# Spectral filter and MLP in one kernel: the real channel folded into the tables, GpSimd's sums taken out, stage 1 and the inverse tables reordered

## The chip, the cores and the metric

The kernel runs on one core of one Trainium2 chip. The metric is device microseconds (us) of one execution, the median of the timed runs. A run has a state; runs over 1.5% above the fastest of the same kernel count as slow, and verdicts and ratios use fast runs alone. That rule turns out to matter here, because the kernel before has two kinds of execution 1.6% apart, for a reason that an experiment below shows.

## The reference

Two blocks with a layernorm ahead of each. The first is a 2-D real FFT of a 2048 x 512 input, a product with complex weights, and the inverse transform; the second is an MLP with a squared ReLU (D = 512, F = 1792).

```python
def _A_ref(x, w_r, w_i):
    X = jnp.fft.rfft2(x.astype(jnp.float32), axes=(-2, -1))
    X = X * (w_r + 1j * w_i)                      # 2048 x 257 complex
    return jnp.fft.irfft2(X, s=(2048, 512), axes=(-2, -1)).astype(jnp.bfloat16)

def _B_ref(x, w1, b1, w2, b2):
    h = x @ w1 + b1
    r = jnp.where(h > 0, h, 0)
    return (r * r) @ w2 + b2

h = x + _A_ref(_layernorm(x), A_w_r, A_w_i)
h2 = h + _B_ref(_layernorm(h), B_w1, B_b1, B_w2, B_b2)
```

A real FFT of 512 points has 257 channels, of which channels 0 and 256 are real. That is one channel too many for 256 complex slots. The kernel before keeps channels 0 to 255 in the slots, leaves the imaginary table of channel 0 at zero and packs the two real channels 0 and 256 into slot 0, which therefore needs a different product from all the others.

## The kernel before

The transforms are matmuls with sine tables made on the chip. Stage 1 (with the layernorm folded into the table `KFr`) and stages 2 and 3 go forward, `spectral` multiplies with the weights, stages 4, 5 and 6 go back; then the MLP runs in five chunks (the "dense part"). The parts that the argument touches:

```python
def ln1_fold(a, b):                                   # layernorm's 1/std into stage 1's table
    for g in range(a, b):
        nc.vector.tensor_scalar(KFr[:, g, :], KF[:], rs1[:, g:g + 1], None, ALU.mult)

def real_products(e, a, b):                           # slot 0: its own products, on GpSimd
    ...
    nc.gpsimd.tensor_tensor(ta[:], SD[:, e], a.unsqueeze(1).to_broadcast([P, 2, 2]), ALU.mult)
    nc.gpsimd.tensor_tensor(tb[:], SD[:, e], b.unsqueeze(1).to_broadcast([P, 2, 2]), ALU.mult)

def real_sums(t, p_out, m_out):                       # ... and sums of 2 elements per partition
    ta, tb = t
    nc.gpsimd.tensor_tensor(p_out, ta[:, 0], tb[:, 1], ALU.subtract)
    nc.gpsimd.tensor_tensor(m_out, ta[:, 1], tb[:, 0], ALU.add)

def spectral(pr):                                     # VectorE: 8 instructions per pair of rows
    ...
    for m, w in ((mA, WB[0]), (mB, WB[1])):
        nc.vector.tensor_tensor(m[:], X[:], w[:, pr:pr + step + 1:step, 0:256]..., ALU.mult)
    ...
    prods = real_products(pr, AB[:, 0, :, 0], AB[:, 1, :, 0])
    nxt[0]()                                          # half of the next pair's butterfly
    nc.vector.tensor_tensor(Z[:, :, 0], mA[:, :, 0], mB[:, :, 1], ALU.subtract)
    nc.vector.tensor_tensor(Z[:, :, 1], mA[:, :, 1], mB[:, :, 0], ALU.add)
    nxt[1]()
    nc.vector.tensor_tensor(M[:, 0], Z[:, 0], Z[:, 1], ALU.add)
    nc.vector.tensor_tensor(M[:, 1], Zf[:, 3::-3], Zf[:, 1:3], ALU.subtract)
    real_sums(prods, M[:, 0, :, 0], M[:, 1, :, 0])    # GpSimd overwrites slot 0 of M

def table_i(*ks):                                     # inverse tables: transpose, copy, negate
    tr = mm_tile("ptr", BF16)
    ...                                               # TensorE transposes EF into tr
    nc.scalar.copy(EI[:, sl, 0:2, :], tr[...])
    if ks[0] == 0: ...                                # KI too
    else: nc.vector.tensor_scalar(EI[:, sl, 2, :], EI[:, sl, 0, :], -1.0, None, ALU.mult)

for pr in range(9):
    if 0 < pr and pr + 2 < 8: stage3(pr + 2)
    if pr + 3 < 8:            stage2(pr + 3)
    if pr > 0:                stage4(pr - 1, split=(pr == 8))     # reads Z and M
    if pr >= 5:               warm(mm_tile("idle")[:, 0:512], 5)
    if pr < 8:                spectral(pr)
    if pr < 3:                table_i(*((0, 8), (1, 2, 3), (4, 5, 6, 7))[pr])
    ...
```

The names: U is stage 2's result and AB stage 3's, each copied from TensorE's output by ScalarE. VectorE's butterfly makes X from AB (sums and differences of the pair's two rows; pair 0 needs none); mA and mB are X times the real and the imaginary weights; Z and M combine them, and stage 4 reads M (for pair 0 also Z). T is stage 4's result. EF and GF are the sine tables of the way forward, EI, KI and GI those of the way back. X, Z and M have two buffers each. KFr is stage 1's table times rs, the layernorm's 1/std.

In the trace before, ScalarE's copies come in the order of this loop (T at 35.13 us, the table EI at 36.04, AB at 36.73), so the place of `table_i` in it is also its place in ScalarE's row.

Of the kernel before, what the change touches and what calls it, by code (L numbers as in the profile page):

```python
# [15 lines left out]
P = 128  # L16
# [18 lines left out]
def kernel(  # L35
# [16 lines left out]

# [32 lines left out]
    SD = fwd.tile([P, 9, 2, 2], FP32, name="SD")  # L85
# [60 lines left out]
    def w_reversed(i):  # L146
# [5 lines left out]
    w_reversed(0)  # L152
# [22 lines left out]
    w_reversed(1)  # L175
    nc.gpsimd.memset(mhalf[:], -0.5)
    nc.gpsimd.iota(idxL[:].rearrange("p (r e j) -> p r e j", r=2, e=2), pattern=[[0, 2], [1, 2], [2, 128]], base=0,
                   channel_multiplier=0)
    nc.gpsimd.memset(idxL[:, 256:257], 256)

    def angles_g(t):
        o = 512 * t
        nc.gpsimd.tensor_scalar(fiG[:, o:o + 257], idxL[:, 0:257], cols[:, t:t + 1], float(QT), ALU.mult, ALU.add)
        nc.gpsimd.tensor_scalar(fiG[:, o + 257:o + 512], idxL[:, 257:512], cols[:, t:t + 1], float(HT),
                                ALU.mult, ALU.add)
# [33 lines left out]
    def ln1_fold(a, b):  # L219
        for g in range(a, b):  # L220
            nc.vector.tensor_scalar(KFr[:, g, :], KF[:], rs1[:, g:g + 1], None, ALU.mult)  # L221

    def stage1(g0, n=0, split=False):
        if split:
            pts = [mm_tile("p1a")[:, 0:512], mm_tile("p1b")[:, 0:512]]
        else:
            pt = mm_tile("p1")
            pts = [pt[:, 0:512], pt[:, 512:1024]]
# [11 lines left out]
        if split:  # L240
            for t, cp in ((0, nc.scalar.copy), (1, nc.vector.tensor_copy)):
                cp(dst[:, 2 * t:2 * t + 2], pts[t].rearrange("p (e i q s) -> p e i q s", e=2, i=2, q=16))  # L242
        else:
            nc.scalar.copy(dst, pt[:].rearrange("p (e i q s) -> p e i q s", e=4, i=2, q=16))  # L244
# [12 lines left out]
    ln1_sums(7)
    angles_g(0)
    ln1_rstd(2, 6)
    ln1_stats(6, 8, 9)  # L260
    ln1_fold(2, 6)
    angles_g(1)
    stage1(2)
    ln1_rstd(6, 10)
    nc.gpsimd.memset(ident[:], 0.0)
    nc.gpsimd.affine_select(out=ident[:], in_=ident[:], compare_op=ALU.not_equal,
                            fill=1.0, base=0, pattern=[[-1, P]], channel_multiplier=1)
    stage1(4)
    ln1_stats(10, 11)
    ln1_fold(6, 10)  # L270
    ln1_rstd(10, 12)
    sin_of(GF[:].rearrange("p t c -> p (t c)"), fiG[:])
    stage1(6)
    ln1_stats(12, 13)
# [20 lines left out]
    def w_real():  # L295

        for e in (0, 8):
            nc.gpsimd.tensor_scalar(SD[:, e, 0, :], WB[0][:, e, 0::256], 0.5, 1.0, ALU.mult, ALU.mult)
            nc.gpsimd.tensor_scalar(SD[:, e, 1, :], WB[1][:, e, 0::256], -0.5, 1.0, ALU.mult, ALU.mult)
        n_r, n_i = (w[:, 1:8, 0::256] for w in WB)  # L300
        v_r, v_i = (w[:, 22:15:-1, 0::256] for w in WB)
        nc.gpsimd.tensor_tensor(SD[:, 1:8, 0, :], n_r, v_r, ALU.add)
        nc.gpsimd.tensor_tensor(SD[:, 1:8, 1, :], v_i, n_i, ALU.subtract)
        nc.gpsimd.tensor_scalar(SD[:, 1:8], SD[:, 1:8], 0.5, 1.0, ALU.mult, ALU.mult)


# [381 lines left out]
```

## Time and profile before

| | us |
|---|---|
| median of 3 runs (188.0, 190.91, 191.0) | 190.91 |
| span of the profiled execution | 189.2 |
| VectorE's first product with the weights (mA of pair 0) | 26.25 |
| VectorE's last M of the spectral part ends | 59.39 |
| first stage 5 matmul (dense part begins) | 61.94 |
| from there to the end | 127.3 |

Rows of a timeline read: start, duration, engine, line, operation, output<-inputs and their shapes, count; in brackets the idle time of the engine just before and what ended it. PE is TensorE, PEld its weight loads, DVE VectorE, ACT ScalarE, POOL GpSimd. A duration can overlap the next instruction's start a little (an X of 0.42 us, and Z 0.34 us after its start), so VectorE's real pace is read from start to start. The "granted clock" is TensorE's clock as a share of full speed.

### The profile page before, as it was taken

The numbers are of one execution on the slowest core, as the hardware profiler recorded it, in microseconds if no ns is written. First come the engines' busy times: TensorE is split into PE (matmuls) and PEld (weight loads), VectorE is DVE, ScalarE is ACT, GpSimd is POOL, SyncE is SP. The second block draws the span as 40 slices with busy tenths as digits, with TensorE's granted clock in tenths as the row PEclk, the third lists the DMA queues.
The fourth block names the chain that finished last, engine by engine and source line by source line (L and its number), as shares of the span: only waits on it lengthen the run. The fifth ranks groups of instructions, "written<-read, shape, count | busy, mean of one in ns | idle before, by whom it ended". The sixth has DMA issues, their size and how long they took to land.

```text
span 189.2 us, 2712 instructions
## 1 busy us (share of the span) xinstructions
PE 160.5 (85%) x935; PEld 89.5 (47%) x948; DVE 124.1 (66%) x302; ACT 100.4 (53%) x169; POOL 63.2 (33%) x127
## 2 busy tenths in 40 slices
PE   3486876983499878799999899999999989999992
PEld 1154654752254447536563355444554434556440
DVE  7898479299686737764789526698436885449421
ACT  4768676995183427714791327860527850348300
POOL 7876946027753024020430202430204332016000
PEclk9999999999799999999999999999999999999999
DMA  5999970000000000001000100000010000110010
GB/s 163 351 410 412 368 179 10 0 0 3 0 2 0 0 0 3 0 2 48 11 0 0 44 12 28 3 0 28 28 59 2 0 0 28 54 35 0 0 55 29
DMA packets 7773, 11.19 MB, mean 59 GB/s; under 512 B 2256, under 2 KB 6224, under 8 KB 7504
## 3 DMA queue, kind: packets, MB, share of 16 engines
q1 hardware_dynamic: 7600, 10.11, 15.6%
q0 software_dynamic: 160, 0.92, 1.2%
q8 instruction: 7, 0.11, 0.3%
q14 instruction: 6, 0.05, 0.1%
HBM read 8.93 MB, written 2.10 MB: 58 GB/s over the span
## 4 chain that ended last, share of the span: by engine, by line
PE 52%; DVE 19%; ACT 16%; POOL 9%; issue 3%; POOLq 0%; ACTq 0%; DVEq 0%
PE ph L593 21%; PE po L612 19%; POOL M L317 3%; DVE act L597 3%; ACT U L341 3%; PE p L496 3%; ACT AB L367 2%; DVE hs L511 2%; ACT rl L596 2%; PE p L555 2%; DVE st L520 2%; ACT Bt L244 2%; ACT T L432 2%; ACT junk L517 1%; POOL rs L528 1%
## 5 line engine op out<-in xcount | busy, mean ns | idle before, releaser
L593 PE MATMUL ph<-UT,W 128*128 128x384 bf16 (+2 forms) x278 | 53.0, 336 | 0.8 <-ACT UT L559 0.5
L596 ACT ACTIVATE rl<-ph,b1f 128x384 bf16<-128x384 f32 (+2 forms) x70 | 41.2, 603 | 20.9 <-PE ph L593 19.5
L612 PE MATMUL po<-W,act 128*128 128x512 bf16 x217 | 49.9, 379 | 0.4
L597 DVE TENSOR_TENSOR act<-rl 128x384 bf16<-128x384 bf16 (+2 forms) x70 | 32.5, 478 | 17.2 <-ACT rl L596 16.8
L600 POOL TENSOR_TENSOR hb<-hs,b2b 128x512 f32<-128x512 bf16 x16 | 18.4, 1153 | 57.4 <-DVE act L597 55.4
L593 PEld LDWEIGHTS <-W 128*128 128x128 bf16 x280 | 27.3, 98 | 20.8 <-issue 1.4
L612 PEld LDWEIGHTS <-act 128*128 128x128 bf16 x224 | 21.6, 98 | 27.3 <-issue 3.1
L616 DVE TENSOR_TENSOR ot<-po,hb 128x512 bf16<-128x512 f32 x16 | 11.0, 690 | 18.1 <-PE po L612 18.1
L540 ACT ACTIVATE u<-hs,nm,rs 128x512 bf16<-128x512 bf16 x6 | 4.7, 809 | 25.2 <-DVE nm L537 25.2
L235 PE MATMUL p<-KFr,xs 128*128 128x256 bf16 x28 | 8.5, 330 | 5.1 <-DVE KFr L221 5.1
L424 PE MATMUL p<-EI,M 128*128 128x256 bf16 x28 | 7.2, 288 | 5.6 <-POOL M L317 5.4
L317 POOL TENSOR_TENSOR M<-ta,tb 128x2 bf16<-128x2 f32 x7 | 7.7, 1101 | 11.4 <-DVE M L406 11.2
L432 ACT CAST T<-p 128x1024 bf16<-128x1024 f32 x7 | 7.3, 1037 | 7.6 <-PE p L425 7.6
L511 DVE SCALAR_TENSOR_TENSOR hs<-p,xs 128x512 bf16<-128x512 f32 x16 | 10.8, 679 | 0.1
L496 PE MATMUL p<-GI,T 128*128 128x256 bf16 x64 | 9.4, 272 | 0.4 <-DVE T L430 0.4
L210 DVE BATCH_NORM_STATS2 st<-xs 128x6 f32<-128x512 bf16 x14 | 9.0, 673 | 0.6 <-DMA xs<-in_A_x_dram 0.6
L244 ACT CAST Bt<-p 128x1024 bf16<-128x1024 f32 x7 | 6.9, 1014 | 4.5 <-PE p L237 4.5
L249 PE MATMUL idle<-ones 128*128 128x512 bf16 x36 | 8.9, 379 | 0.1
L334 PE MATMUL p<-GF,Bt 128*128 128x256 bf16 x64 | 8.1, 273 | 0.8 <-ACT Bt L242 0.8
L510 PE MATMUL p<-R,KI 128*128 128x512 bf16 x16 | 6.1, 380 | 3.2 <-DVE R L506 3.1
L237 PE MATMUL p<-KFr,xs 128*128 128x256 bf16 x28 | 8.7, 335 | 0.0
L527 POOL TENSOR_SCALAR rs<-mv 128x3 f32<-128x3 f32 (+2 forms) x5 | 1.2, 240 | 22.3 <-DVE mv L521 22.2
(153 smaller groups left out, 237.0 us busy)
## 6 DMA issues: line engine op xcount, KB each, us to landing
W<-in_B_w_dram SPq DMA_DIRECT2D x2, 1792.0 KB, 19.0
out_dram<-ot SPq DMA_DIRECT2D x16, 128.0 KB, 1.8
xs<-in_A_x_dram SPq DMA_DIRECT2D x3, 512.0 KB, 6.9
WB<-in_A_w_r_dram SPq DMA_DIRECT2D x1, 1028.0 KB, 12.1
WB<-in_A_w_i_dram SPq DMA_DIRECT2D x1, 1028.0 KB, 12.9
xs<-in_A_x_dram SPq DMA_DIRECT2D x2, 256.0 KB, 3.5
b2b<-in_B_b_dram SPq DMA_DIRECT2D x1, 128.0 KB, 8.3
WB<-in_A_w_r_dram,idxR POOLq DMA_INDIRECT x1, 9.2
```

The source lines that it names most:

```text
L210: nc.vector.bn_stats(st[:], xs[:, g, :])
L244: nc.scalar.copy(dst, pt[:].rearrange("p (e i q s) -> p e i q s", e=4, i=2, q=16))
L317: nc.gpsimd.tensor_tensor(p_out, ta[:, 0], tb[:, 1], ALU.subtract)
L432: nc.scalar.copy(dst, src)
L496: nc.tensor.matmul(pe[:, 256 * e:256 * e + 256], lhsT=T2[:, lt, g].rearrange("p q s -> p (q s)"), rhs=GI[:, lt, :], start=(r == 0), stop=( ...
L511: nc.vector.scalar_tensor_tensor(hs[:, g, :], py[:], WSC, xs[:, g, :], ALU.mult, ALU.add)
L593: nc.tensor.matmul(ph[:, 0:n], lhsT=W1[:, d, bass.ts(f, P)], rhs=UT[:, d, 0:n], start=(d == 0), stop=(d == ND - 1))
L596: nc.scalar.activation(rl[:, 0:n], ph[:, 0:n], ACT.Relu, bias=b1f[:, f:f + 1], scale=1.0)
L597: sq = nc.vector.tensor_tensor(act[:, f, 0:n], rl[:, 0:n], rl[:, 0:n], ALU.mult)
L600: add = nc.gpsimd.tensor_tensor(hb[:, g, :], hs[:, g, :], b2b[:], ALU.add)
L612: nc.tensor.matmul(po[:], lhsT=act[:, f, bass.ts(i, P)], rhs=W2[:, f, :], start=(f == 0), stop=(f == NF - 1))
L616: nc.vector.tensor_tensor(ot[:], po[:], hb[:, g, :], ALU.add)
```

## The change

Its intent: use channels 1 to 256 as the 256 slots, so that channel 256 is an ordinary slot (its table column is halved) and channel 0, which the layernorm's mean subtraction makes zero on the input side, needs none. Then slot 0 needs no product of its own, and GpSimd leaves the spectral part. In the same edit stage 1 is reordered, one more group's statistics go to ScalarE (three instead of two), two folds go to GpSimd, and the inverse tables are copied earlier. Not shown in this excerpt: as the slots shift by one, even and odd channels swap places in the matmuls of stages 2 and 5. The diffs here are condensed; some put several lines into one.

```diff
-    w_reversed(0)                                   # gathers of the reversed weight rows, on GpSimd
+    nc.gpsimd.iota(idxL[...], ..., base=1, ...)     # channels 1 to 256
 ...
-def ln1_fold(a, b):
+def ln1_fold(a, b, eng=nc.vector):
 ...
     ln1_sums(3)
+    ln1_sums(7)
     ln1_stats(0, 1)
     ln1_rstd(0, 2)
+    w_reversed(0)
 ...
-    ln1_sums(7)
+    ln1_sums(11)
     angles_g(0)
     ln1_rstd(2, 6)
+    w_reversed(1)
 ...
     ln1_rstd(6, 10)
+    ln1_fold(8, 10, nc.gpsimd)
+    angles_g(1)
     stage1(4)
-    ln1_stats(10, 11)
-    ln1_fold(6, 10)
+    ln1_stats(10, 12)
+    ln1_fold(6, 8)
 ...
-    nc.vector.memset(GF[:, :, 0:1], 0.0)
+    nc.vector.tensor_scalar(GF[:, :, 255:256], GF[:, :, 255:256], 0.5, None, ALU.mult)
-    stage1(14, split=True)
+    tr08 = stage1(14, split=True)                   # free half of its PSUM buffer
+    transposed(tr08, (0, 8), True)
+    nc.scalar.copy(KI[:], tr08[:, 4 * P:5 * P])
+    table_i(tr08, (0, 8))
 ...
-    def w_real(): ...
-    def real_products(e, a, b): ...
-    def real_sums(t, p_out, m_out): ...
 ...
-            nc.vector.tensor_tensor(m[:], X[:], w[:, pr:pr + step + 1:step, 0:256]..., ALU.mult)
+            nc.vector.tensor_tensor(m[:], X[:], w[:, pr:pr + step + 1:step, 1:Df]..., ALU.mult)
-            prods = real_products(pr, AB[:, 0, :, 0], AB[:, 1, :, 0])
-            real_sums(prods, M[:, 0, :, 0], M[:, 1, :, 0])
 ...
     stage2(2)
-    w_real()
+    tr = mm_tile("ptr", BF16)
+    transposed(tr, (1, 2, 3))
+    table_i(tr, (1, 2, 3))
     stage3(2)
 ...
-        if pr < 3:
-            table_i(*((0, 8), (1, 2, 3), (4, 5, 6, 7))[pr])
+        if pr == 0:
+            table_neg((1, 3))
+            tr = mm_tile("ptr", BF16)
+            transposed(tr, (4, 5, 6, 7))
+            table_i(tr, (4, 5, 6, 7))
+        if pr == 1:
+            table_neg((4, 7))
```

More of the change, by code (lines that the diff above doesn't have):

```diff
@@ L84 @@
     WB = [fwd.tile([P, 23, Df], BF16, name=f"WB{i}") for i in range(2)]
-    SD = fwd.tile([P, 9, 2, 2], FP32, name="SD")
     KF = fwd.tile([P, 256], BF16, name="KF")
@@ L150, in w_reversed @@
             in_offset=bass.IndirectOffsetOnAxis(ap=idxR[:, 0:1], axis=0))
-    w_reversed(0)
+    nc.gpsimd.iota(idxL[:].rearrange("p (r e j) -> p r e j", r=2, e=2), pattern=[[0, 2], [1, 2], [2, 128]], base=1,
+                   channel_multiplier=0)
+    nc.gpsimd.memset(mhalf[:], -0.5)
     nc.vector.tensor_single_scalar(pI[:, 1:2], pI[:, 0:1], 3, ALU.arith_shift_right)
@@ L174 @@
     nc.gpsimd.tensor_scalar(fiE[1][:], fiE[0][:], 1.0, float(QT), ALU.mult, ALU.add)
-    w_reversed(1)
-    nc.gpsimd.memset(mhalf[:], -0.5)
-    nc.gpsimd.iota(idxL[:].rearrange("p (r e j) -> p r e j", r=2, e=2), pattern=[[0, 2], [1, 2], [2, 128]], base=0,
-                   channel_multiplier=0)
-    nc.gpsimd.memset(idxL[:, 256:257], 256)
     def angles_g(t):
         o = 512 * t
-        nc.gpsimd.tensor_scalar(fiG[:, o:o + 257], idxL[:, 0:257], cols[:, t:t + 1], float(QT), ALU.mult, ALU.add)
-        nc.gpsimd.tensor_scalar(fiG[:, o + 257:o + 512], idxL[:, 257:512], cols[:, t:t + 1], float(HT),
-                                ALU.mult, ALU.add)
+        for r, q in ((0, QT), (256, HT)):
+            nc.gpsimd.tensor_scalar(fiG[:, o + r:o + r + 256], idxL[:, r:r + 256], cols[:, t:t + 1], float(q),
+                                    ALU.mult, ALU.add)
     def table_e(i):
@@ L217, in ln1_rstd @@
         nc.gpsimd.tensor_tensor(rs1[:, a:b], rs1[:, a:b], mhalf[:, 0:b - a], ALU.pow)
-    def ln1_fold(a, b):
+    def ln1_fold(a, b, eng=nc.vector):
         for g in range(a, b):
-            nc.vector.tensor_scalar(KFr[:, g, :], KF[:], rs1[:, g:g + 1], None, ALU.mult)
+            eng.tensor_scalar(KFr[:, g, :], KF[:], rs1[:, g:g + 1], None, ALU.mult)
     def stage1(g0, n=0, split=False):
         if split:
-            pts = [mm_tile("p1a")[:, 0:512], mm_tile("p1b")[:, 0:512]]
+            two = [mm_tile("p1a"), mm_tile("p1b")]
+            pts = [pt[:, 0:512] for pt in two]
         else:
@@ L242, in stage1 @@
                 cp(dst[:, 2 * t:2 * t + 2], pts[t].rearrange("p (e i q s) -> p e i q s", e=2, i=2, q=16))
+            return two[0][:, 512:1024].bitcast(BF16)
         else:
@@ L249, in warm, with transposed, table_i, table_neg @@
             nc.tensor.matmul(o, lhsT=ones[:, 0:P], rhs=ones[:], start=True, stop=True)
+    def transposed(o, ks, kf=False):
+        for j, k in enumerate(ks):
+            for i in range(2):
+                nc.tensor.transpose(o[:, P * (2 * j + i):P * (2 * j + i) + P], EF[:, k, i, :], ident[:])
+        if kf:
+            nc.tensor.transpose(o[:, 2 * P * len(ks):2 * P * len(ks) + P], KF[:, 0:P], ident[:])
+    def table_i(o, ks):
+        n, sl = len(ks), slice(ks[0], ks[-1] + 1, ks[1] - ks[0])
+        nc.scalar.copy(EI[:, sl, 0:2, :], o[:, 0:2 * P * n].rearrange("p (a k b) -> p a k b", a=n, k=2))
+    def table_neg(ks):
+        nc.vector.tensor_scalar(EI[:, ks[0]:ks[-1] + 1, 2, :], EI[:, ks[0]:ks[-1] + 1, 0, :], -1.0, None, ALU.mult)
     ln1_sums(3)
+    ln1_sums(7)
     ln1_stats(0, 1)
     ln1_rstd(0, 2)
+    w_reversed(0)
     ln1_stats(2, 4, 5)
@@ L256 @@
     stage1(0, 8)
-    ln1_sums(7)
+    ln1_sums(11)
     angles_g(0)
     ln1_rstd(2, 6)
+    w_reversed(1)
     ln1_stats(6, 8, 9)
     ln1_fold(2, 6)
-    angles_g(1)
     stage1(2)
     ln1_rstd(6, 10)
-    nc.gpsimd.memset(ident[:], 0.0)
-    nc.gpsimd.affine_select(out=ident[:], in_=ident[:], compare_op=ALU.not_equal,
-                            fill=1.0, base=0, pattern=[[-1, P]], channel_multiplier=1)
+    ln1_fold(8, 10, nc.gpsimd)
+    angles_g(1)
     stage1(4)
-    ln1_stats(10, 11)
-    ln1_fold(6, 10)
-    ln1_rstd(10, 12)
+    ln1_stats(10, 12)
+    ln1_fold(6, 8)
     sin_of(GF[:].rearrange("p t c -> p (t c)"), fiG[:])
     stage1(6)
-    ln1_stats(12, 13)
+    ln1_rstd(10, 12)
+    ln1_stats(13)
     ln1_rstd(12, 14)
@@ L279 @@
     ln1_rstd(14, 16)
+    nc.gpsimd.memset(ident[:], 0.0)
+    nc.gpsimd.affine_select(out=ident[:], in_=ident[:], compare_op=ALU.not_equal,
+                            fill=1.0, base=0, pattern=[[-1, P]], channel_multiplier=1)
     stage1(10)
@@ L282 @@
     stage1(12)
+    ln1_fold(14, 16)
     nc.vector.tensor_scalar(EF[:, :, 2, :], EF[:, :, 0, :], -1.0, None, ALU.mult)
-    nc.vector.memset(GF[:, :, 0:1], 0.0)
-    ln1_fold(14, 16)
-    stage1(14, split=True)
-    nc.gpsimd.tensor_scalar(cols[:, 4:5], pF[:, 0:1], 256.0, None, ALU.mult)
-    nc.gpsimd.tensor_scalar(cols[:, 5:6], pF[:, 0:1], 256.0, 128.0, ALU.mult, ALU.add)
+    nc.vector.tensor_scalar(GF[:, :, 255:256], GF[:, :, 255:256], 0.5, None, ALU.mult)
[3 more added lines that the diff above has]
+    table_i(tr08, (0, 8))
+    nc.gpsimd.tensor_scalar(cols[:, 4:5], pF[:, 0:1], 256.0, 128.0, ALU.mult, ALU.add)
+    nc.gpsimd.tensor_scalar(cols[:, 5:6], pF[:, 0:1], 256.0, 256.0, ALU.mult, ALU.add)
     nc.gpsimd.iota(idxD[:], pattern=[[1, 256]], base=0, channel_multiplier=0)
@@ L293 @@
                                 float(HT if lt // 2 else QT), ALU.mult, ALU.add)
-    def w_real():
-        for e in (0, 8):
-            nc.gpsimd.tensor_scalar(SD[:, e, 0, :], WB[0][:, e, 0::256], 0.5, 1.0, ALU.mult, ALU.mult)
-            nc.gpsimd.tensor_scalar(SD[:, e, 1, :], WB[1][:, e, 0::256], -0.5, 1.0, ALU.mult, ALU.mult)
-        n_r, n_i = (w[:, 1:8, 0::256] for w in WB)
-        v_r, v_i = (w[:, 22:15:-1, 0::256] for w in WB)
-        nc.gpsimd.tensor_tensor(SD[:, 1:8, 0, :], n_r, v_r, ALU.add)
-        nc.gpsimd.tensor_tensor(SD[:, 1:8, 1, :], v_i, n_i, ALU.subtract)
-        nc.gpsimd.tensor_scalar(SD[:, 1:8], SD[:, 1:8], 0.5, 1.0, ALU.mult, ALU.mult)
-    def real_products(e, a, b):
-        ta = fwd.tile([P, 2, 2], FP32, tag="ta", bufs=4, name="ta")
-        tb = fwd.tile([P, 2, 2], FP32, tag="tb", bufs=4, name="tb")
-        nc.gpsimd.tensor_tensor(ta[:], SD[:, e], a.unsqueeze(1).to_broadcast([P, 2, 2]), ALU.mult)
-        nc.gpsimd.tensor_tensor(tb[:], SD[:, e], b.unsqueeze(1).to_broadcast([P, 2, 2]), ALU.mult)
-        return ta, tb
-    def real_sums(t, p_out, m_out):
-        ta, tb = t
-        nc.gpsimd.tensor_tensor(p_out, ta[:, 0], tb[:, 1], ALU.subtract)
-        nc.gpsimd.tensor_tensor(m_out, ta[:, 1], tb[:, 0], ALU.add)
     GFv = GF[:].rearrange("p t (r e j) -> p t r e j", r=2, e=2)
-    Us, Xs, ABs, BSs, Zs, Ms = {}, {}, {}, {}, {}, {}
+    Us, Xs, ABs, Zs, Ms = {}, {}, {}, {}, {}
     def stage2(pr, split=False):
@@ L333, in stage2 @@
                 for t in range(2):
-                    nc.tensor.matmul(puv[:, :, e, :], lhsT=Bt[:, 2 * t + e, 2 * pr + q, :], rhs=GFv[:, t, :, e, :],
+                    nc.tensor.matmul(puv[:, :, e, :], lhsT=Bt[:, 2 * t + 1 - e, 2 * pr + q, :], rhs=GFv[:, t, :, e, :],
                                      start=(t == 0), stop=(t == 1))
@@ L351, in stage3 @@
                 nc.tensor.matmul(o, lhsT=C, rhs=U[:, u, :], start=True, stop=False)
-                nc.tensor.matmul(o[:, 1:256], lhsT=Sp, rhs=U[:, u, 257:512], start=False, stop=False)
-                nc.tensor.matmul(o[:, 257:512], lhsT=Sn, rhs=U[:, u, 1:256], start=False, stop=True)
-                nc.tensor.matmul(pxs[u][:, 512:514], lhsT=Sp, rhs=U[:, u, 0::256], start=True, stop=True)
-            BSs[pr] = bs = fwd.tile([P, 2, 2], FP32, name="bs")
+                nc.tensor.matmul(o[:, 0:256], lhsT=Sp, rhs=U[:, u, 256:512], start=False, stop=False)
+                nc.tensor.matmul(o[:, 256:512], lhsT=Sn, rhs=U[:, u, 0:256], start=False, stop=True)
             for u, cp in ((0, nc.scalar.copy), (1, nc.vector.tensor_copy)):
                 cp(X[:, u].rearrange("p r c -> p (r c)"), pxs[u][:, 0:512])
-                cp(bs[:, u], pxs[u][:, 512:514])
         else:
@@ L385, in spectral @@
         for m, w in ((mA, WB[0]), (mB, WB[1])):
-            nc.vector.tensor_tensor(m[:], X[:], w[:, pr:pr + step + 1:step, 0:256].unsqueeze(2).to_broadcast([P, 2, 2, 256]), ALU.mult)
+            nc.vector.tensor_tensor(m[:], X[:], w[:, pr:pr + step + 1:step, 1:Df].unsqueeze(2).to_broadcast([P, 2, 2, 256]), ALU.mult)
         Zs[pr] = Z = fwd.tile([P, 2, 2, 256], BF16, tag="Z", bufs=2, name="Z")
         Ms[pr] = M = fwd.tile([P, 2, 2, 256], BF16, tag="M", bufs=2, name="M")
-        if pr == 0:
-            bs = BSs.pop(pr)
-            prods = [real_products(8 * u, X[:, u, :, 0], bs[:, u]) for u in range(2)]
-        else:
-            AB = ABs.pop(pr)
-            prods = real_products(pr, AB[:, 0, :, 0], AB[:, 1, :, 0])
+        ABs.pop(pr, None)
         nxt[0]()
@@ L401, in spectral @@
             nc.vector.tensor_copy(M[:, :, 1], Z[:, :, 0])
-            for u in range(2):
-                real_sums(prods[u], Z[:, u, :, 0], M[:, u, :, 0])
         else:
@@ L432, in stage4 @@
             nc.scalar.copy(dst, src)
-    def table_i(*ks):
-        tr = mm_tile("ptr", BF16)
-        n, sl = len(ks), slice(ks[0], ks[-1] + 1, ks[1] - ks[0])
-        for j in range(2 * n):
-            nc.tensor.transpose(tr[:, P * j:P * j + P], EF[:, ks[j // 2], j % 2, :], ident[:])
-        nc.scalar.copy(EI[:, sl, 0:2, :], tr[:, 0:2 * P * n].rearrange("p (a k b) -> p a k b", a=n, k=2))
-        if ks[0] == 0:
-            nc.tensor.transpose(tr[:, 2 * P * n:2 * P * n + P], KF[:, 0:P], ident[:])
-            nc.scalar.copy(KI[:], tr[:, 2 * P * n:2 * P * n + P])
-        else:
-            nc.vector.tensor_scalar(EI[:, sl, 2, :], EI[:, sl, 0, :], -1.0, None, ALU.mult)
     stage2(0, split=True)
@@ L464 @@
             spectral(pr)
-        if pr < 3:
-            table_i(*((0, 8), (1, 2, 3), (4, 5, 6, 7))[pr])
+        if pr == 0:
[5 more added lines that the diff above has]
+            table_neg((4, 7))
         if pr == 4:
             sin_of(GI[:].rearrange("p t c -> p (t c)"), fiI[:])
-            nc.gpsimd.memset(GI[0:1, 2, 0::2], 1.0)
-            nc.gpsimd.memset(GI[0:1, 2, 1::2], -1.0)
             nc.gpsimd.tensor_copy(b1f[:], b1b[:])
@@ L495, in s5 @@
                 lt = 2 * r + e
-                nc.tensor.matmul(pe[:, 256 * e:256 * e + 256], lhsT=T2[:, lt, g].rearrange("p q s -> p (q s)"),
+                nc.tensor.matmul(pe[:, 256 - 256 * e:512 - 256 * e], lhsT=T2[:, lt, g].rearrange("p q s -> p (q s)"),
                                  rhs=GI[:, lt, :], start=(r == 0), stop=(r == 1))
```

## The prediction

> **What bounds the kernel now.** I read the page first, then the chain that ended last, then the table of busy time by stage, then each engine's timeline up to 62 us. From the page and the table: from about 62 us on (the dense part) TensorE is the bound. It is busy 160.5 of 189.2 us in all and between 94% and 99% from 80 to 170 us. The change doesn't touch those matmuls. The spectral part before it is different: no engine is full there and the bound passes from one to another. Busy time by stage (each engine's busy us and instruction count, granted clock, DMA share, GB/s):
>
> ```profile
> 35.00:40.00 5.00, 4.87 (x42) 3.42 (x41) 3.12 (x9) 5.00 (x7) 0.00 (x0) 1.00 0.00 0
> 40.00:45.00 5.00, 3.57 (x27) 2.45 (x26) 4.84 (x13) 4.67 (x6) 2.42 (x5) 1.00 0.01 3
> 45.00:50.00 5.00, 0.05 (x1) 0.05 (x1) 4.83 (x13) 0.52 (x1) 5.00 (x3) 0.95 0.00 0
> 50.00:55.00 5.00, 5.00 (x25) 2.86 (x26) 2.61 (x6) 3.55 (x4) 2.14 (x12) 0.71 0.00 2
> ```
>
> The columns after the length are PE, PEld, DVE, ACT, POOL. In 45 to 50 us TensorE does one instruction, ScalarE half a microsecond; VectorE is full and GpSimd "busy" 5.00 us with three instructions. The chain says what everybody waits for (start, us, what):
>
> ```profile
> 43.31 0.43 DVE M L406
> 43.87 6.03 POOL M L317
> 49.95 0.40 PE p L424
> ```
>
> GpSimd's sum for the real channel writes two elements per partition of M, and stage 4 reads M. The timelines show what is wrong with it:
>
> ```profile
> 43.87 6.02 POOL L317 TENSOR_TENSOR M<-ta,tb 128x2 bf16<-128x2 f32 x1 [2.37 <-DVE M L406]
> ...
> 49.41 0.42 DVE L377 TENSOR_TENSOR X<-AB 128x512 bf16<-128x512 bf16 x1
> 49.85 0.20 POOL L318 TENSOR_TENSOR M<-ta,tb 128x2 bf16<-128x2 f32 x1
> 49.95 0.10 PEld L424 LDWEIGHTS <-M 128*128 128x128 bf16 x1 [5.71 <-POOL M L317]
> 49.95 0.40 PE L424 MATMUL p<-EI,M 128*128 128x256 bf16 x1 [5.43 <-POOL M L317]
> 50.14 0.42 PE L425 MATMUL p<-EI,M 128*128 128x256 bf16 x1
> ```
>
> The same 2-element sum takes 0.25 us at 40.20, when VectorE has a gap, and 6.02 us here. VectorE runs tensor_tensor without a gap from 40.76 to 49.83, and the GpSimd instruction ends 0.06 us after VectorE stops. So the "busy" 6.02 us is a wait. Two more waits of the spectral part matter, one on VectorE's row and two at the end of stage 1:
>
> ```profile
> 36.88 0.29 DVE L445 TENSOR_SCALAR EI<-EI 128x384 bf16<-128x384 bf16 x1 [3.96 <-ACT EI L440]
> ```
> ```profile
> 19.03 0.28 PE L235 MATMUL p<-KFr,xs 128*128 128x256 bf16 x1 [1.68 <-DVE KFr L221]
> ...
> 20.11 1.93 ACT L244 CAST Bt<-p 128x1024 bf16<-128x1024 f32 x2 [0.88 <-PE p L237]
> ```
>
> VectorE stands 3.96 us because it must negate the inverse table before pair 2's products, and ScalarE copies that table late (36.04). TensorE stands 1.68 us and then ScalarE 0.88 us because VectorE does the statistics of groups 12 to 15 ahead of the fold of groups 10 and 11.
>
> [...] after 5.43 us idle the 256-column matmuls take 0.42 us until 51.2 against 0.27 before, and the granted clock of 50 to 55 us is 0.71. [...] the weights are now read from column 1 instead of 0, with rows of 257 elements. [...] odd pairs start on an odd element already (row 1 is element 257) and their product with the weights takes 0.69 us (29.46), as the even pairs' does (26.25, 37.09). The shift only swaps which pairs are odd; I count nothing for it.
>
> **The change part by part.** *Real channel folded away.* Out go GpSimd's 9 products on each side and 9 + 9 sums (L311, L312, L317, L318: 0.8 + 2.3 + 0.9 + 2.2 + 1.5 + 7.7 + 2.6 = 18.0 us in the page and its groups), 7 SD preparations, two 2-element copies on ScalarE and VectorE, two 2-column matmuls. No GpSimd instruction is left between the tables and b1f[...]. The wait of TensorE (5.43) and its slow clock afterwards go.
>
> *Tables earlier.* The first inverse table's transposes go into the free half of a stage 1 buffer; ScalarE copies it before stage 2's results exist. The second (pairs 1 to 3) is copied before pair 2's AB, the third after spectral(0). VectorE's two negations keep 0.2 us each but find their data ready: ScalarE's copy of pairs 1 to 3 should end near 28.1, VectorE comes to it at 28.3.
>
> *Stage 1.* ScalarE takes group 11 too (2 activations and 2 accumulator reads, about 1.4 us, in a gap that group 7 used; group 7 moves to the gap 8.4 to 11.0). VectorE loses one bn_stats (0.66); GpSimd takes two folds of 256 elements (estimate 0.55 each, from its 0.57 us for 257 elements of fiG). Statistics of 7 no longer hold rs[6:10] to 13.65. The fold of 10 and 11 comes near 17.0 instead of 18.72, so TensorE runs stage 1 without the 1.68 us wait. But ScalarE's evictions are the bound from 15.45: what is won is its 0.88 us idle and a little more, 1.0 us. ScalarE then ends stage 1 near 21.5 (22.53 now), copies KI and EI (0.2 + 0.5) while stage 2's matmuls run, so these are hidden. With the bs copies out (0.15), mA of pair 0 starts at 26.25 - 1.15 = 25.1.
>
> *Spectral part after the change.* What is left is VectorE's own work. One pair is 47.20 - 43.98 = 3.22 us start to start, pair 0 is 29.46 - 26.25 = 3.21, the last has no butterfly: 2 x 0.61 + 4 x 0.335 + tail = 2.65. Sum: 3.21 + 6 x 3.22 + 2.65 + 2 x 0.2 = 25.6 us. From 25.1 it ends at 50.7; now it ends at 59.39. **Gain 8.7 us**: 1.15 at the start and 33.1 - 25.6 = 7.5 us of waits between. Is another engine slower than that? ScalarE per pair: AB, U and T, 3 x 0.905 start to start = 2.7; GI's sine 0.95 once. TensorE per pair: stages 2, 3, 4, 0.86 each = 2.6, warm. Both are under 3.22. I stepped ScalarE's order through by hand: AB of pairs 2, 3, 4, 5 ends near 29.4, 32.1, 34.9, 37.6, and VectorE needs them at 29.75, 33.2, 36.4, 39.6. Slack 0.3 us at first, growing.
>
> *Dense part.* M's end to the first s5 matmul is 2.55 us (59.39 to 61.94) and stays. The odd half of s5 now comes second and od is copied from the first half, so ScalarE may start 0.2 us sooner, once on the path. From there 127.3 us unchanged.
>
> Sum: 8.7 + 0.2 = 8.9, less an allowance of 0.4 for small new waits (the slack of 0.3 above): 8.5 us. 190.91 - 8.5 = **182.4 us**.
>
> **Rivals.** (1) ScalarE takes the place of GpSimd: between 25 and 36 us it has the same copies as VectorE has products and 0.3 us slack. In the trace before it ran without a gap from 33.30 to 43.27. If each of the first three pairs waits 0.5 us for AB, the time is about 184. (2) [...] VectorE finds another wait for the 3.96; about 185. Against it: ScalarE's late copy at 36.04 is a matter of order, which the diff changes. (3) GpSimd's two new folds or the gathers, moved from 3.07 and 5.88 to about 7.2 and 10.7, [...] and stage 2 slips: against it, GpSimd's work from 9 to 19 us keeps its normal durations (0.7 to 1.04 for a power) beside bn_stats. The gathers took 9 us to land; from 11.7 they land by 21, and are needed at 28.5. It would cost 1 to 2 us: 184. (4) The stall is a lottery: one of the three runs before took 188.0, so perhaps it is often 3 us shorter. That makes the gain smaller against such runs but not the time after.
>
> **Range and chances.** The gain stands on VectorE's measured 3.22 us; misses are mostly upward. Rivals 1 to 3 end at 184 to 185; if all hidden gains come, 181.5; another 1.5 us either way is run to run. 80%: 180.0 to 185.5. Faster by over 2% means below 187.1: 0.96; same 0.03; slower 0.01.
>
> **What would show it.** Right: no GpSimd row between 23 and 50 us but b1f; VectorE without idle over 0.3 us from 25 to 51; the first s5 matmul near 53; TensorE's matmuls in stage 4 all near 0.27 us; ScalarE's stage 1 end near 21.5; dense part 127 us. Wrong: VectorE idle before X waiting for AB (rival 1), before EI (rival 2), stage 2 later than 22.6 (rival 3), [...] or a dense part longer than 128 us.

## The result

| | before | after |
|---|---|---|
| median of the timed runs beside each other | 189.59 us (188.0, 188.28, 190.91, 191.0) | 183.74 us (183.66 to 183.80) |
| span profiled | 189.2 | 181.9 |
| mA of pair 0 starts | 26.25 | 26.44 |
| last M ends | 59.39 | 52.07 |
| first stage 5 matmul | 61.94 | 54.56 |
| from there to the end | 127.3 | 127.3 |

A ratio here is the mean time of one kernel's fast runs over that of the other's of the same rounds, so not quite the ratio of the medians quoted. It is 0.9764 (0.9745 to 0.9783), which is the ratio to the runs of 188.0 and 188.28 alone (183.73 / 188.14 = 0.977): the runs of 191 lie over 1.5% above the fastest and don't count. In a later series, in which all runs of the kernel before were between 190.9 and 191.7, the ratio for the same two kernels was 0.9598 (0.9581 to 0.9615).

The table of busy time of the changed kernel over the stretch where the one before stood still (columns as above):

```profile
30.00:35.00 5.00, 4.04 (x42) 2.97 (x40) 5.00 (x14) 4.80 (x6) 0.00 (x0) 1.00 0.00 0
35.00:40.00 5.00, 4.69 (x37) 3.48 (x36) 5.00 (x13) 4.52 (x6) 0.00 (x0) 1.00 0.00 0
40.00:45.00 5.00, 4.38 (x31) 2.87 (x30) 5.00 (x14) 4.76 (x6) 0.00 (x0) 1.00 0.01 3
45.00:50.00 5.00, 4.77 (x33) 2.93 (x32) 5.00 (x13) 3.47 (x4) 0.00 (x0) 1.00 0.00 2
```

VectorE is busy 5.00 of 5.00 us four times in a row, GpSimd does nothing, and the granted clock stays at 1.00. From 45 to 50 us TensorE is busy 4.77 us, where it was 0.05 before. All that VectorE waited for between 24 and 52 us (engine, line, waited for: total us, times, longest):

```profile
DVE U L335 <- PE p L330: 1.2, 1, 1.2
DVE X L351 <- PE p3b L349: 1.1, 1, 1.1
DVE mA L379 <- DVE X L351: 0.5, 1, 0.5
```

The waits for the table and for ScalarE's AB are gone from this list; what is left lies ahead of the first product. The timeline of the end of stage 1 shows the part that did not come as predicted, first GpSimd, then VectorE, ScalarE and TensorE:

```profile
13.88 1.93 POOL L216 TENSOR_SCALAR KFr<-KF,rs 128x256 bf16<-128x256 bf16 x2
15.90 0.94 POOL L179 TENSOR_SCALAR fiG<-idxL,cols 128x256 int32<-128x256 int32 x2
```
```profile
17.99 0.48 DVE L216 TENSOR_SCALAR KFr<-KF,rs 128x256 bf16<-128x256 bf16 x2 [1.27 <-POOL rs L212]
```
```profile
16.86 1.06 ACT L113 ACTIVATE GF<-fiG 128x1024 bf16<-128x1024 int16 x1 [0.84 <-POOL fiG L179]
17.83 3.77 ACT L241 CAST Bt<-p 128x1024 bf16<-128x1024 f32 x4
```
```profile
18.34 0.28 PE L231 MATMUL p<-KFr,xs 128*128 128x256 bf16 x1 [1.61 <-DVE KFr L216]
...
22.14 0.40 PE L251 MATMUL p1a<-ident,EF 128*128 128x128 bf16 x4 [0.53 <-ACT Bt L238]
```

GpSimd's two folds take 1.93 us, then come the angles, which ScalarE waits 0.84 us for, then rs of groups 10 and 11, which VectorE waits 1.27 us for. TensorE's wait ahead of groups 10 and 11 is 1.61 us where it was 1.68: the order changed, the wait stayed, with GpSimd as its cause in VectorE's place. The new transposes then wait 0.53 us for ScalarE.

### The profile page after: what moved, and what is told of

The parts are those of the page before. It is cut to its first block, busy times and chain, and to the rows that moved or that the text cites. A ratio compares the mean times of both kernels' runs of the same rounds, so it can differ in the third digit from the quotient of the medians.

```text
span 181.9 us, 2667 instructions
## 1 busy us (share of the span) xinstructions
PE 160.0 (88%) x946; PEld 89.0 (49%) x946; DVE 122.2 (67%) x297; ACT 101.8 (56%) x172; POOL 46.5 (26%) x83
## 4 chain that ended last, share of the span: by engine, by line
PE 50%; DVE 29%; ACT 9%; POOL 6%; issue 4%; DVEq 0%; POOLq 0%; ACTq 0%
PE ph L570 22%; PE po L589 20%; DVE act L574 3%; PE p L473 3%; DVE mA L379 3%; DVE mB L379 3%; DVE hs L488 2%; ACT rl L573 2%; ACT Bt L241 2%; PE p L532 2%; DVE st L497 2%; DVE st L205 2%; DVE M L392 2%; DVE Z L384 2%; ACT junk L494 1%
## 5 line engine op out<-in xcount | busy, mean ns | idle before, releaser
L589 PE MATMUL po<-W,act 128*128 128x512 bf16 x224 | 50.8, 379 | 0.0
L574 DVE TENSOR_TENSOR act<-rl 128x384 bf16<-128x384 bf16 (+2 forms) x70 | 32.5, 477 | 17.2 <-ACT rl L573 16.9
L502 POOL TENSOR_TENSOR nm<-mv 128x1 f32<-128x1 f32 x5 | 1.5, 291 | 30.9 <-ACT junk L494 30.9
L246 PEld LDWEIGHTS <-ones 128*128 128x128 bf16 x45 | 4.7, 106 | 7.8 <-POOL ones L142 2.9
L205 DVE BATCH_NORM_STATS2 st<-xs 128x6 f32<-128x512 bf16 x13 | 8.3, 673 | 0.0
L360 ACT CAST AB<-p 128x1024 bf16<-128x1024 f32 x7 | 7.1, 1014 | 1.9 <-PE p L358 1.2
L473 PEld LDWEIGHTS <-T 128*128 128x128 bf16 x64 | 6.2, 98 | 3.5 <-ACT T L414 0.9
```

What stands on the lines that cost most here:

```text
L205: nc.vector.bn_stats(st[:], xs[:, g, :])
L246: nc.tensor.matmul(o, lhsT=ones[:, 0:P], rhs=ones[:], start=True, stop=True)
L473: nc.tensor.matmul(pe[:, 256 - 256 * e:512 - 256 * e], lhsT=T2[:, lt, g].rearrange("p q s -> p (q s)"), rhs=GI[:, lt, :], start=(r == 0), ...
L574: sq = nc.vector.tensor_tensor(act[:, f, 0:n], rl[:, 0:n], rl[:, 0:n], ALU.mult)
L589: nc.tensor.matmul(po[:], lhsT=act[:, f, bass.ts(i, P)], rhs=W2[:, f, :], start=(f == 0), stop=(f == NF - 1))
```

## The experiments

Twelve runs of eleven kernels (the kernel before twice, the changed one once more, nine variants), all correct and all profiled in the fast state. "Stage 5" is the start of the first stage 5 matmul in the profile; from there to the end it is 127.3 to 127.4 us in every one of the twelve, so this start is the whole difference in span. Against the kernel before of the same rounds the verdict is "faster" for e5 to e9 and a0, "same" for e0 and "unclear" for e1 to e4 and e0b: there the runs of the kernel before lay at 188 and at 191 and were counted together. So e1 to e4 are compared with each of its two groups.

| run | median us (lowest to highest) | stage 5 |
|---|---|---|
| e0_before | 191.01 (190.96 to 191.71) | 62.63 |
| e0b_before | 188.26 (188.1 to 190.9) | 58.98 |
| e1_fold | 188.01 (187.4 to 188.03) | 58.88 |
| e2_tables | 188.73 (188.71 to 189.38) | 59.61 |
| e3_fold_tables | 183.84 (183.82 to 183.84) | 54.72 |
| e4_sums_on_vector | 188.88 (188.58 to 188.94) | 59.84 |
| e5_unread | 184.15 (184.13 to 184.17) | 55.02 |
| e6_rewritten | 185.33 (185.3 to 185.36) | 56.23 |
| e7_rewritten_vector | 184.16 (184.13 to 184.19) | 55.01 |
| a0_after | 183.69 (183.68 to 183.74) | 54.62 |
| e8_stage1_order | 182.23 (181.95 to 182.34) | 53.21 |
| e9_order_and_late_tables | 181.98 (181.96 to 182.22) | 53.10 |

The theory at the outset: two hold-ups of the spectral part, GpSimd's sum of 6.02 us and the late table, are worth about 8 us together, and the new stage 1 is worth nothing. The rivals: only one of the two counts; the sum costs because of the dependence or the work and not because it is on GpSimd; the spread of the kernel before lies elsewhere.

### The parts one by one: e1_fold, e2_tables, e3_fold_tables

**e1_fold** takes the folded channel alone.

```diff
-    real_sums(prods, M[:, 0, :, 0], M[:, 1, :, 0])   # and all that belongs to the fold, as in the change
 # stage 1's order and table_i's places as before
```

> Only the folded real channel; stage 1 and the order of the tables as before. My theory: the two hold-ups are separate. VectorE still waits about 4 us for the inverse table of pairs 1 to 3 (to near 36.8 us), then runs without a gap: 36.9 + 0.2 + 5 x 3.22 + 0.2 + 2.65 = 56.0 us against 59.39 before, so the first matmul of stage 5 near 58.5 and about 187.5 us against a before of 191 (the kind of run that was profiled). Rival [...]: the whole stall goes, about 184. Rival (ScalarE is behind anyway): 189 or more.

Measured 188.01 us, stage 5 at 58.88. VectorE's timeline has the wait for the table as before, and after it only a second one of 0.17 us:

```profile
36.69 0.29 DVE L424 TENSOR_SCALAR EI<-EI 128x384 bf16<-128x384 bf16 x1 [4.03 <-ACT EI L419]
40.36 0.29 DVE L424 TENSOR_SCALAR EI<-EI 128x512 bf16<-128x512 bf16 x1 [0.17 <-ACT EI L419]
```

VectorE's last M ends at 56.4 us, against 56.0 expected. The rival "the whole stall of 6 us goes, 184" falls: with the table late, taking GpSimd out wins 3 us on an execution of 191 and nothing on one of 188.

**e2_tables** takes the earlier tables alone.

```diff
+    tr08 = stage1(14, split=True); transposed(tr08, (0, 8), True); ...   # the tables as in the change
 # real_products, real_sums and stage 1's order as before
```

> Only the earlier tables; GpSimd's sums and stage 1 as before. My theory: the wait of 4 us for the table goes, [...] so the gain is lost again: a GpSimd sum of 5 us or more that TensorE waits for, and a time within 2 us of before (188 to 192). Rival (the waits simply add): 4 us faster than before, about 187 or 184.5 by the kind of run of before.

Measured 188.73 us: slower than a good execution of the kernel before (188.0 to 188.3), although the wait of 4 us is gone. My theory was right in the total and wrong in one detail. GpSimd's timeline:

```profile
46.71 4.11 POOL L486 CAST b1f<-b1b 128x14 f32<-128x14 bf16 x1
50.78 0.20 POOL L331 TENSOR_TENSOR ta<-SD,AB 128x4 f32<-128x4 f32 x1
50.93 0.38 POOL L332 TENSOR_TENSOR tb<-SD,AB 128x4 f32<-128x4 f32 x1
51.39 0.26 POOL L337 TENSOR_TENSOR M<-ta,tb 128x2 bf16<-128x2 f32 x1
```

This time no sum is long. A small cast of a bias takes 4.11 us, where it took 0.27 in the trace after (28.53), and the next sum queues behind it. TensorE waits 3.99 us for that sum, and the stages behind it then have to catch up.

**e3_fold_tables** takes both, with stage 1 in its old order.

```diff
-    ln1_fold(8, 10, nc.gpsimd)
+    # stage 1 as before: gathers at 2.9 and 5.9 us, group 11's statistics and all folds on VectorE
```

> The changed kernel with the stage 1 order of before. My theory from the trace after: the reordering of stage 1 is worth nothing, since GpSimd's two folds (0.97 us each) and two gathers (1.2 us each) took the place of VectorE's delay; so 183.7 within 0.5 us, VectorE's first product with the weights near 26.0 to 26.5. Rival (the prediction on record): it is worth 1 us, so 184.7.

Measured 183.84 us against 183.69 to 183.74 for the whole change: the new stage 1 is worth 0.1 to 0.15 us. The four versions make a table (us):

| | GpSimd's sums | folded away |
|---|---|---|
| tables late | 188.0 to 188.3, or 190.9 to 192.2 | 188.01 |
| tables early | 188.73 | 183.84 |

The two parts don't add up: each alone ends near 188 to 189, both together at 183.84. With the table late, VectorE stands 4 us anyway. With it early, VectorE runs without a gap from 27.98 to 50.76 us, and in e2's profile four of GpSimd's sums took 0.25 us each beside that stream (33.04 to 42.92 us) before the cast took 4.11, to 50.82. Of the four versions only the one with the table early and nothing on the path on GpSimd any more has the whole gain.

### Is it that the sum is on GpSimd? e4_sums_on_vector, e5_unread, e6_rewritten, e7_rewritten_vector

**e4_sums_on_vector** is the kernel before with the last sums moved; the products stay on GpSimd.

```diff
-    nc.gpsimd.tensor_tensor(p_out, ta[:, 0], tb[:, 1], ALU.subtract)
-    nc.gpsimd.tensor_tensor(m_out, ta[:, 1], tb[:, 0], ALU.add)
+    nc.vector.tensor_tensor(p_out, ta[:, 0], tb[:, 1], ALU.subtract)
+    nc.vector.tensor_tensor(m_out, ta[:, 1], tb[:, 0], ALU.add)
```

> The kernel before with the real channel's last sums on VectorE instead of GpSimd: same arithmetic, same dependence of stage 4 on it[...] (the products stay on GpSimd and may still be late). My theory: the 6 us sum goes although no work is folded away; 18 small VectorE instructions cost about 0.1 us each: 58 us for the first stage 5 matmul, 187.5 to 189. [...] Rival (the cost was the extra work or the dependence[...]): no faster than before, 190 to 192.

Measured 188.88 us, with all four runs within 0.4 us. The arithmetic and the dependence are those of before, and none of the four executions is one of 191, where five of seven of the kernel before were in the same rounds. It is 0.6 to 0.9 us slower than an execution of before that has no stall: VectorE has 18 more instructions, and two of them lengthen a pair from 3.22 to 3.42 us. One of the products left on GpSimd took 2.52 us (30.79), but VectorE waited for none of them.

**e5_unread** adds to the changed kernel one GpSimd sum per pair that nobody reads.

```diff
+            pq = fwd.tile([P, 2], BF16, tag="pq", bufs=8, name="pq")
+            nc.gpsimd.tensor_tensor(pq[:], Z[:, 0, :, 0], Z[:, 1, :, 0], ALU.add)
```

> The changed kernel plus one GpSimd sum of 2 elements in each of pairs 1 to 7, whose result nobody reads. My theory: [...] at least one of the seven takes over 5 us (as many as 10 to 20 us: VectorE has no gap from 26 to 50 us), none of it matters to anyone, and the time stays at 183.7 within 0.5 us. Rival (a GpSimd sum delays VectorE by its own 0.2 us, or the 6 us was an accident): all seven near 0.25 us; time up by 1 us or so.

The durations, from the tile's own view (count: least/median/longest ns):

```profile
L396 POOL TENSOR_TENSOR pq<-Z x7: 191/311/5746, 32.0 to 51.7; 128x2 bf16<-128x2 bf16 x7
```

The longest of seven sums of two elements takes 5.75 us with only the cast of b1f besides for GpSimd to do; others took 2.72 and 2.19, the rest 0.2 to 0.3. The expectation of 10 to 20 us was too high, and the time is up 0.46 us over a0_after (184.15 against 183.69), inside the limit that I had set but not nothing. Both have to do with what ends a long sum:

```profile
38.80 5.90 POOL L396 TENSOR_TENSOR pq<-Z 128x2 bf16<-128x2 bf16 x2 [2.91 <-DVE Z L385]
```
```profile
44.07 0.42 DVE L369 TENSOR_TENSOR X<-AB 128x512 bf16<-128x512 bf16 x1
44.58 0.42 DVE L384 TENSOR_TENSOR Z<-mA,mB 128x512 bf16<-128x512 bf16 x1
```

Each of the three long sums ends 0.03 to 0.05 us before a Z of VectorE (34.74, 44.58, 50.89) that starts late: 0.51, 0.51 and 0.80 us after the instruction before it, where a0_after has 0.34, 0.34 and 0.74. That is 0.40 us in all; the short sums show no such delay. For the longest the buffers offer a reason: it reads the Z of pair 3, and the late Z of pair 5 needs that buffer. For the other two the reason stays open.

**e6_rewritten** makes stage 4 wait for such a sum (it rewrites the same values), and **e7_rewritten_vector** does the same on VectorE.

```diff
 e6:
+            nc.gpsimd.tensor_tensor(M[:, 0, :, 0], Z[:, 0, :, 0], Z[:, 1, :, 0], ALU.add)
 e7:
+            nc.vector.tensor_tensor(M[:, 0, :, 0], Z[:, 0, :, 0], Z[:, 1, :, 0], ALU.add)
```

> The changed kernel with GpSimd writing M's first column once more in pairs 1 to 7 (same values, so the output stays right): stage 4 waits for it. My theory: stage 4 stops until VectorE runs out of buffers and pauses, a GpSimd sum takes 5 us or more, and the time rises by 3 to 8 us to 187 to 192. Rival [...]: under 1 us more.

> The same rewriting of M's first column, by VectorE: same dependence[...]. My theory: seven more VectorE instructions of some 0.1 us each on the bound: 0.5 to 0.9 us more, 184.2 to 184.6. Rival [...]: as much as the one on GpSimd.

e6 measured 185.33 us, 1.6 more than a0_after; e7 184.16, 0.5 more and just under the 184.2 to 184.6 expected. So the work and the dependence cost about 0.5 us on VectorE, and putting them on GpSimd adds 1.2. e6's longest sum, one of seven of the same shape, took 5.02 us, but TensorE waited only 1.76 us for it:

```profile
44.65 0.28 PE L410 MATMUL p<-EI,M 128*128 128x256 bf16 x1 [1.76 <-POOL M L395]
```

The expectation of 3 to 8 us for e6 was too high. Of the 5.02 us of its longest sum, 1.76 reached TensorE. The longest GpSimd instruction of these profiles was the sum of pair 3 in e5, in e6 and in the kernel before (5.75, 5.02 and 6.02 us), and the cast of b1f in e2 (4.11); what decides where is not shown.

### Why the kernel before has two times: e0_before, e0b_before

Both are the kernel before, unchanged.

> The kernel before once more, for the spread: its four timed runs were 188.0, 188.3, 190.9 and 191.0 us. My theory: [...] a run of 188 has a longest sum about 3 us shorter than the 6.02 us of the run of 191, and the dense part is 127.3 us in both. Rival: the spread lies in the dense part or in the start.

> The kernel before a third time. Of its timed runs so far some lie at 188.0 to 188.3 us and most at 190.9 to 192.2; both profiles were of the slow kind, each with a GpSimd sum of 6.02 us. My theory: should the profile fall on a run of 188, [...] the rest is the same; if it falls on a run of 191 it shows 6.02 us again and tells nothing. Rival: a profile of 188 with a sum of 6.02 us, the difference lying in the dense part.

e0_before's profile fell on an execution of 191.7 us and showed the sum of 6.02 us again. It adds one thing: stage 5 begins 0.69 us later than in the first profile, and the granted clock from 50 to 55 us was 0.50 there and 0.71 in the first. This fits the smaller steps between 190.9 and 191.7 being set by how long TensorE stays slow after the standstill; two profiles are few to show it.

In both, the standstill ends itself. The sum of 6.02 us belongs to pair 3, whose stage 4 waits for it. VectorE runs on until the M of pair 5, which needs the buffer that pair 3's M still holds, and there it has to wait for stage 4. The sum ends at 49.89 us, 0.06 after that pause begins (first profile):

```profile
51.51 0.42 DVE L406 TENSOR_TENSOR M<-Z 128x512 bf16<-128x512 bf16 x1 [1.68 <-PE p L425]
```

So the 6 us are about as long as the two buffers of M let VectorE run ahead: from the M of pair 3 at 43.31 to 49.83 us. While the sum ran, 14 VectorE instructions of 0.42 to 0.69 us each started.

e0b_before's profile fell on an execution of 188.1. GpSimd's sums in the tile's own view, first of the stalled profile of the kernel before, then of this one:

```profile
L317 POOL TENSOR_TENSOR M<-ta,tb x7: 202/252/6023, 32.7 to 59.2; 128x2 bf16<-128x2 f32 x7
```
```profile
L317 POOL TENSOR_TENSOR M<-ta,tb x7: 249/252/253, 32.5 to 56.2; 128x2 bf16<-128x2 f32 x7
```

None of these seven is over 0.26 us. I had expected a sum about 3 us shorter; instead the stall is absent altogether. What is 3 us shorter is its effect: stage 5 begins at 58.98 instead of 61.94, and the rest is 127.3 us in both. The wait for the table (3.96 us at 36.67) is in both. So in the profiles at hand the spread of the kernel before, 188 or 191, is this one GpSimd instruction taking 6.02 us or 0.25. What decides it in an otherwise equal execution stays open: in both it starts 0.56 us after VectorE's first M of the same pair (L406) does: 43.87 after 43.31 in the stalled profile, 43.66 after 43.10 in this one. And VectorE's next instruction follows 0.11 us later in both:

```profile
43.66 0.25 POOL L317 TENSOR_TENSOR M<-ta,tb 128x2 bf16<-128x2 f32 x1 [2.36 <-DVE M L406]
```
```profile
43.77 0.68 DVE L386 TENSOR_TENSOR mA<-X,WB 128x1024 bf16<-128x1024 bf16 x1
```

The short sum here needs no gap. VectorE's stream has none from 40.55 to 54.7 us in this profile, four of the sums run in it in 0.25 us each, and VectorE keeps its 3.22 us a pair. Beside a stream without gaps the sum of pair 3 took 6.02 us in one execution and 0.25 us in another.

### Stage 1: a0_after, e8_stage1_order, e9_order_and_late_tables

**a0_after** is the changed kernel once more, for the same chip and rounds.

> The changed kernel once more, beside the two that follow on the same chip: 183.7 us within 0.3, the first stage 5 matmul at 54.6, VectorE's first product with the weights at 26.44 after an idle of 0.5 us if that wait is tied to this program, without it if it was an accident of one execution.

183.69 us. The idle of 0.50 us ahead of mA of pair 0 is there again, as in all profiles with this stage 1 (also e5, e6 and e7), and in none with another.

**e8_stage1_order** takes load off GpSimd and in the same edit reorders VectorE's folds and statistics.

```diff
-    nc.gpsimd.iota(idxL[...]); nc.gpsimd.memset(mhalf[:], -0.5)
+    nc.gpsimd.memset(mhalf[:], -0.5); w_reversed(0)         # gather in GpSimd's gap at 2.9 us
 ...
     ln1_rstd(0, 2)
-    w_reversed(0)
+    w_reversed(1)
 ...
-    angles_g(0); ln1_rstd(2, 6); w_reversed(1)
-    ln1_stats(6, 8, 9); ln1_fold(2, 6); stage1(2)
-    ln1_rstd(6, 10); ln1_fold(8, 10, nc.gpsimd); angles_g(1)
+    ln1_rstd(2, 6); angles_g(0)
+    ln1_stats(6, 8); ln1_fold(2, 4); stage1(2)
+    ln1_stats(9); ln1_fold(4, 6); ln1_rstd(6, 10); angles_g(1)
 ...
-    ln1_fold(6, 8)
+    ln1_fold(6, 8); ln1_fold(8, 10)
 ...
-    ln1_stats(14, 15); ln1_fold(10, 12)
+    ln1_fold(10, 12); ln1_stats(14, 15)
```

> The changed kernel with stage 1 in another order: the first gather back in GpSimd's gap at 2.9 us, the second between two powers, the folds of groups 8 and 9 back on VectorE, groups 2 and 3 folded before the statistics of 9, groups 10 and 11 before those of 14 and 15. My theory: what ate the gain predicted for stage 1 was GpSimd, busy 9.2 of 10 us from 10 to 20 us. Freed of 1.9 us of folds and 1.2 us of a gather it delivers the angles of GF and rs of 10 and 11 earlier, ScalarE's last eviction of stage 1 ends near 20 instead of 22.1, and the whole kernel gains 1.5 to 2.5 us: 181.3 to 182.3. Rival (the loads bound the start: all runs begin the first product with the weights near 26.3, when the loads end): stage 1 ends earlier, but VectorE then waits before the first product, and the time stays within 0.5 us of 183.7.

Measured 182.23 us, 0.9519 of before, where a0_after is 0.9598 in the same rounds: 1.5 us won, the lower end of what was expected. ScalarE's and VectorE's timelines:

```profile
14.87 1.07 ACT L113 ACTIVATE GF<-fiG 128x1024 bf16<-128x1024 int16 x1
15.83 2.84 ACT L242 CAST Bt<-p 128x1024 bf16<-128x1024 f32 x3
19.21 1.01 ACT L242 CAST Bt<-p 128x1024 bf16<-128x1024 f32 x1 [0.54 <-PE p L234]
20.11 0.59 ACT L239 CAST Bt<-p1a 128x512 bf16<-128x512 f32 x1
```
```profile
24.78 0.70 DVE L381 TENSOR_TENSOR mA<-X,WB 128x1024 bf16<-128x1024 bf16 x1
```

GF's sine waits for nobody, VectorE's waits for GpSimd's rs in stage 1 come to 1.1 us instead of 3.5, ScalarE ends stage 1 at 20.70 instead of 22.09, and mA starts at 24.78 with no idle before it. How much of this is GpSimd's load and how much VectorE's order was not tested one by one. TensorE's clock is not the reason: its matmuls of stage 1 take 0.42 us instead of 0.27 until 14.8 us in the profile of the changed kernel, until 16.9 in a0_after and until 12.8 in e8, and between the first two stage 5 differs by only 0.06 us. (The granted clock of the first profile reads 1.00 there all the same; the durations are the safer sign.) The rival that the loads hold the start near 26.3 us falls. ScalarE still waits 0.54 us, for groups 12 and 13, whose fold now stands behind the statistics of 14 and 15.

**e9_order_and_late_tables** also moves the transposes of tables 0 and 8 out of the end of stage 1.

```diff
-    transposed(tr08, (0, 8), True)
-    nc.scalar.copy(KI[:], tr08[:, 4 * P:5 * P])
-    table_i(tr08, (0, 8))
 ...
             transposed(tr, (4, 5, 6, 7))
+            transposed(tr[:, 1024:2048], (0, 8))
             table_i(tr, (4, 5, 6, 7))
+            table_i(tr[:, 1024:2048], (0, 8))
+        if pr == 6: ...                             # KF's transpose and KI's copy
```

> As the one before, and the transposes of tables 0 and 8 moved from the spare half of the last stage 1 buffer to the third table's buffer, since in the trace after they wait 0.53 us for ScalarE's eviction of that buffer and hold stage 2 up by 0.4 us. My theory: another 0.4 us gained, 181.0 to 182.0; ScalarE is later by 0.5 us before AB of pair 3, which may cost VectorE up to 0.3 us. Rival (stage 2 is not what counts): within 0.1 us of the one before or slower.

Measured 181.98 us. The medians differ by 0.25 us and the ranges of the two overlap (181.95 to 182.34, 181.96 to 182.22), so no gain is shown, and the rival that stage 2's start is not what counts stays open; stage 5 begins 0.11 us earlier in the profiles. Without the transposes the first stage 2 matmul waits 0.27 us for the same eviction, and the second group 0.23 us for VectorE's:

```profile
20.64 0.28 PE L329 MATMUL p<-GF,Bt 128*128 128x256 bf16 x1 [0.27 <-ACT Bt L239]
21.16 1.81 PE L329 MATMUL p<-GF,Bt 128*128 128x256 bf16 x15 [0.23 <-DVE Bt L239]
```

e8 and e9 are the versions that beat both kernels; 182.0 us is what the study ends with.

## Why the prediction was right

182.4 us was predicted, with 180.0 to 185.5; 183.74 was measured. Step by step:

- **What bounds the spectral part after the change.** Right: VectorE's own work was put at 25.6 us from the first product to the last M; it ran 26.44 to 52.07, 25.63 us, with no wait inside. That it agrees to 0.03 us is luck. Pair 0 took 2.97 us and not 3.21: the trace before, from which 3.21 was read, has VectorE wait 0.16 us for AB inside it (27.71). The last pair took 2.94 us and not 2.65; in the trace before it took 3.01. The two errors cancel. The predicted slack of ScalarE's AB of 0.3 us for pair 2 held, so rival 1 (ScalarE) didn't come true.
- **GpSimd's long sum.** Right that the 6.02 us were a wait and not work, and that they go with GpSimd: a sum of the same size that nobody reads took 0.19 to 5.75 us in one profile (e5), rewriting M's column costs 1.2 us more on GpSimd than on VectorE (e6 against e7), and with the sums on VectorE none of four executions is one of 191 (e4). What keeps such a sum waiting is not shown. But the prediction read the 5.43 us wait as if every execution had it. e0b_before shows executions without, and there the folded channel alone wins nothing (188.01 against 188.0 to 188.3). So the predicted gain of 8.5 us could hold against the stalled kind alone. Rival 4, the lottery, is what happens, with the stall all there or not there rather than 3 us shorter. The time after was not touched by that, as the rival said; the gain is 7.2 us against one kind of execution and 4.3 to 4.5 against the other.
- **The table.** Right that 4 us were a matter of order: 188.01 to 183.84 when the table comes early after the fold. Rival 2, that VectorE finds another wait for the 3.96 us, is refuted: with GpSimd's sums gone and the table late e1 takes 188.01, and in the trace after no other wait takes the place of the 3.96. What the prediction did not see is that either part alone wins little (e1, e2).
- **Stage 1.** The term of the sum that was mis-sized. The prediction had mA start 1.15 us earlier, at 25.1; it started at 26.44, 0.2 us later than before. That this 1.34 us is just the miss of the time, 183.74 - 182.4, is chance. In the sum the 0.4 us allowed for small waits takes up part of it, so stage 5 began 0.9 us late: at 54.56, where 61.94 - 8.7 + 0.4 = 53.64. The other 0.4 us of the miss are the od's 0.2, which did not come, and roundings; besides, the gain was read from an execution of 191.03 us and taken off a median of 190.91. Two of the prediction's own signs failed with this term: VectorE stood 0.50 us ahead of mA, and ScalarE's end of stage 1 was not near 21.5. The 1.34 us have three pieces in the trace after. ScalarE ended stage 1 at 22.09 instead of 21.5 (0.6), because the folds on GpSimd, estimated at 0.55 us each from an int32 instruction, took 0.97, and GpSimd's two gathers were not counted on the path of the powers: this was rival 3, by way of GpSimd's own queue (busy 9.16 us of the 10 from 10 to 20 us). Two folds of 128x256 in bf16 took 1.93 us where two int32 instructions of the same size took 0.94; VectorE ran beside the folds, and whether it has a share in that is not separated. The transposes, to which the prediction gave no time (it called the copies behind them hidden), started stage 2 0.34 us after ScalarE's end where it was 0.06 before (0.3); moving them away showed no gain (e9). And mA waited 0.50 us. Less load on GpSimd together with another order on VectorE gave 1.5 us back (e8). The source of the 0.50 us is not settled: it comes with this stage 1 in five profiles of five and with no other, but no run isolates it.
- **The weights from column 1.** Right that it costs nothing: mA takes 0.675 to 0.696 us for all eight pairs after the change, 0.678 to 0.693 before, over even and odd starts in both.
- **od 0.2 us earlier.** Not seen: from the last M to stage 5 it is 2.49 us instead of 2.55, and ScalarE's first od starts 0.64 us after stage 5 instead of 0.68. Too small to test.
- **The dense part.** Right: 127.3 us, unchanged.

The number was close because its largest term was read from VectorE's own pace, which none of the rivals touched, and because the errors beside it partly cancelled.

## What to carry to other kernels

Before moving small work off a busy VectorE to an idle GpSimd, ask whether anything on the path waits for it: a sum of two elements took 0.25 us or 6 us beside the same unbroken stream of VectorE, and the traces don't show what decides which. In the kernel before, the 6.02 us were about as long as the two buffers of M let VectorE run ahead (43.31 to 49.83 us). When two waits lie one behind the other, test their removal as a two-by-two table, since each alone can win nothing against a good execution while both together win 4 to 7 us. And when a kernel's times fall in two groups, get a profile of each before giving a cause for the gap.
